# First gate and value weights converted inside the attention plan, in the last head pair's buffers

## The chip, the cores and the metric

The kernel runs on one core of a Trainium2 chip. The time is device microseconds (us) of one execution. An engine is named as in the profile: PE is the matrix engine (PEld its weight loads), DVE the vector engine, ACT the scalar engine, POOL the GpSimd engine, SP the engine that issues the DMAs. Each engine executes its own list of instructions from top to bottom, and waits at an instruction until what it needs is done.

## The reference, cut to what matters

```python
# attention: q, k, v are (2, 8, 1152, 64); queries are averaged in pairs
q_pool = q.reshape(B, H, S // 2, 2, D).mean(axis=3)
attn = softmax(q_pool @ k.T / sqrt(D));  attn_out = attn @ v
x = attn_out.transpose(0, 2, 1, 3).reshape(1152, 512)
# first mixture layer: w_gate, w_val are 512 x 1536, w_out is 1536 x 512, all float64
x = (sigmoid(x @ w_gate) * (x @ w_val)) @ w_out
# second layer: 8 experts, w1 512 x 1024, w2 1024 x 512, routing by 8 rounds of normalisation
out = sum(P[:, e:e+1] * (maximum(x @ w1[e], 0) @ w2[e]) for e in range(8))
```

## The kernel before

**Precision.** Every operand of a matmul is held as two words, a rounded high one and a low one with the rest. A product takes three matmuls (`three`, L902 to L905): high by high, high by low of the moving side, low weight by high. In the profile these three are L903, L904 and L905.

**Stages.** The attention runs over 8 head pairs of 9 query tiles each; PE turns and multiplies, DVE takes maxima and splits the turned probabilities (pT, L523), ACT exponentiates and copies, POOL rescales and writes the outputs as high and low words into x1 (tiles of four, one for each 128 columns of x; the last pair writes the last one). Then the gate and value stage runs over 12 blocks of 128 columns (`fc`). A block is 72 matmuls: 36 for the gate into one psum tile psb, 36 for the value into another (two such tiles in all, so block fc+1 uses those of block fc again). ACT takes the sigmoid of the first psb (L942), DVE multiplies it with the second psb (sg, L943), ACT writes the high word of the product (gt, L946) and POOL the low word (gt, L947). Then come the product with w_out and the eight experts.

**Converting float64 weights.** The weights arrive as 64-bit numbers and are turned into two float32 words by `split_doubles` (L184 to L217), for each of gate and value: ACT scales the upper halves (dv, L204), DVE cuts out the sign (ds, L205) and shifts (dv, L206), ACT rounds to the high word (w_gv, L210), DVE subtracts (da, L211), masks (dv, L212) and scales the lower halves (ds, L214), POOL adds both into the low word (w_gv, L217). Five DVE instructions, two of ACT, one of POOL. The results lie in a ring of two weight tiles; `dv` lies in SBUF for block 0 and in psum for the others.

**What sets the order.** The attention's instructions are steps with planned costs and due times; `arrange` (from L225) takes them one after the other by the earliest modelled start, hands out buffers of `stock`, and writes each engine's list in that order (L891 to L896). A step may be taken ahead of its turn by at most AHEAD = 8 units, one unit being a query tile. The gate and value stage is written as plain loops; there the framework's scheduler orders each engine's list by the priority of program order and its own estimates. Block 0's conversion has a raised priority (HP and HO, L923), by which it is mixed into the end of the attention.

Of the kernel before, what the change touches and what calls it, by code (L numbers as in the profile page):

```python
# [8 lines left out]
F32 = mybir.dt.float32  # L9
F32R = mybir.dt.float32r  # L10
I32 = mybir.dt.int32
U32 = mybir.dt.uint32
AF = mybir.ActivationFunctionType
ALU = mybir.AluOpType
AX = mybir.AxisListType
PSUM = bass.MemoryType.PSUM
P = 128
SIGN = -(1 << 31)
SIGNEXP = -(1 << 23)
RINGB = 2  # L20
RT0 = 24
RTS = 12
HP = 1
HO = 30
WA = 336
AHEAD = 8.0
SHIFT = {
# [99 lines left out]
def moe_stack_kernel(ctx: ExitStack, tc: tile.TileContext, q, k, v, wg1, wv1, wo1, wg2, w1, w2, out):  # L127
# [6 lines left out]
    nc = tc.nc  # L134
    B, H, S, D = q.shape
    SP = S // 2
    N, DM = out.shape
    wg1, wv1, wo1 = (w.bitcast(I32) for w in (wg1, wv1, wo1))
    FF = wo1.shape[0]
    E, _, FE = w1.shape  # L140
    KD = DM // P
    NJ = S // P
    NP = H // 2
# [6 lines left out]
    TB = N // 3  # L150
# [13 lines left out]
    def f(ap):  # L164
        return ap.bitcast(F32)
# [15 lines left out]
        j = eng.tensor_tensor(out=out[:, 1], in0=src, in1=f(out[:, 0]), op=ALU.subtract).ins  # L181
        return i, j

    def split_doubles(w, srcs, name, psum=None):  # L184

        for i, src in enumerate(srcs):
            raw = rawp.tile([P, 512, 2], I32, tag="raw", name=f"raw_{name}{i}")
            nc.sync.dma_start(out=raw.rearrange("p (a c) w -> p a (c w)", a=src.shape[1]), in_=src)
            low, high = raw[:, :, 0], raw[:, :, 1]
            a = conv.tile([P, 512], F32, tag="da", name=f"da_{name}{i}")
            s = conv.tile([P, 512], I32, tag="ds", name=f"ds_{name}{i}")
            if psum:
                v = psum.tile([P, 512], F32, tag="dv", name=f"dv_{name}{i}")
            else:  # L200
                v = conv.tile([P, 512], F32, tag="dv", name=f"dv_{name}{i}")
            vi = v.bitcast(I32)

            nc.scalar.activation(out=v, in_=f(high), func=AF.Copy, scale=2.0 ** -112)  # L204
            nc.vector.tensor_scalar(out=s, in0=vi, scalar1=SIGN, scalar2=None, op0=ALU.bitwise_and)  # L205
            nc.vector.scalar_tensor_tensor(  # L206
                out=vi, in0=vi, scalar=3, in1=s, op0=ALU.logical_shift_left, op1=ALU.bitwise_or
            )
            sl = slice(i * 512, (i + 1) * 512)
            nc.scalar.activation(out=w[:, 0, sl], in_=v, func=AF.Copy)  # L210
            nc.vector.tensor_tensor(out=a, in0=v, in1=f(w[:, 0, sl]), op=ALU.subtract)  # L211
            nc.vector.tensor_scalar(out=vi, in0=vi, scalar1=SIGNEXP, scalar2=None, op0=ALU.bitwise_and)  # L212
            t = f(s)
            nc.vector.scalar_tensor_tensor(  # L214
                out=t, in0=low.bitcast(U32), scalar=2.0 ** -52, in1=v, op0=ALU.mult, op1=ALU.mult
            )
            nc.gpsimd.tensor_tensor(out=w[:, 1, sl], in0=a, in1=t, op=ALU.add)  # L217

    x_p = ctx.enter_context(tc.tile_pool(name="x", bufs=1, reuse_waits="tile"))
    conv = ctx.enter_context(tc.tile_pool(name="conv", bufs=2, reuse_waits="tile"))  # L220
# [82 lines left out]
    U = 2 * QT + 1  # L303

    with ExitStack() as pa:
        ld = pa.enter_context(tc.tile_pool(name="ld", bufs=1, reuse_waits="tile"))
# [36 lines left out]
        have = {}  # L343
        steps = {}

        def step(name, eng, when, takes, lasts, emit, deps=(), takes_buf=(), frees=(), after=()):


            entry(steps, name, eng, when, takes, lasts, emit, deps, takes_buf, frees, after)
# [255 lines left out]
        for i in range(B * NP):  # L605
# [59 lines left out]
            for part in range(3):  # L665
                t = (-8.85, -1.45, -2.5)[part] if i == 0 else t0 - 8 + (0.4, 0.8, 0.0)[part]
                n = QT if part < 2 else 1
                made = ("pq", i, part if i == 0 or part == 2 else 3)
                if (i, part) == (0, 0):

                    for x, ts in enumerate((range(1), range(1, QT))):
                        c, w, tt = slice(ts[0] * P, (ts[-1] + 1) * P), len(ts) * P, t + 0.05 * x
# [30 lines left out]
            for j in range(2):  # L703
# [43 lines left out]
                t = t0 + 4.5 + 4 * j  # L747
# [140 lines left out]
            "wl", "POOL", t + 0.001, 150, 200,  # L888
            lambda: nc.gpsimd.tensor_tensor(out=wgs[:, :, 1], in0=wg2_sb, in1=f(wgs[:, :, 0]), op=ALU.subtract), ["wh"],
        )  # L890
        engines = {nc.tensor.engine, nc.vector.engine, nc.scalar.engine, nc.gpsimd.engine, nc.sync.engine}  # L891
        with tc.manual_schedule(engines=engines):
            for s in arrange(steps, stock, AHEAD):
                for what, kind, slot in s["got"]:
                    have[what] = stock[kind][slot]
                s["emit"]()  # L896


    rawp = ctx.enter_context(tc.tile_pool(name="raw", bufs=3, reuse_waits="tile"))
# [17 lines left out]
    with ExitStack() as pb:  # L917
        ring = pb.enter_context(tc.tile_pool(name="ring", bufs=RINGB, reuse_waits="tile"))
        g_p = pb.enter_context(tc.tile_pool(name="g", bufs=1, reuse_waits="tile"))
        gs = []  # L920
        for fc in range(NFF):
            w = ring_tile(f"gv{fc}")[:, :, 0:1024]
            with (tc.high_priority(offset=HO) if fc < HP else ExitStack()):  # L923
                split_doubles(
                    w,
                    [src[:, fc * 2 * P:(fc + 1) * 2 * P].rearrange("(c p) f -> p c f", p=P) for src in (wg1, wv1)],
                    f"gv{fc}", ps_v if fc else None,
                )
            wr = w.rearrange("p s (i c f) -> p s i c f", i=2, c=KD)
            pss = []  # L930
            for i in range(2):
                ps = ps_b.tile([P, 3, 512], F32, tag="b", name="psb")
                for c in range(KD):
                    for n in range(3):
                        cols = slice(n * TB, (n + 1) * TB)
                        three(
                            ps[:, n, 0:TB], wr[:, 0, i, c], wr[:, 1, i, c],
                            x1[c][:, 0, cols], x1[c][:, 1, cols], c == 0, c == KD - 1,
                        )
                pss.append(ps)  # L940
            sg = misc.tile([P, 3, TB], F32, tag="m", name="sg")
            nc.scalar.activation(out=sg, in_=pss[0][:, :, 0:TB], func=AF.Sigmoid)  # L942
            nc.vector.tensor_tensor(out=sg, in0=pss[1][:, :, 0:TB], in1=sg, op=ALU.mult)  # L943
            gt = g_p.tile([P, 2, N], F32R, tag=f"g{fc}", name="gt")
            sgf = sg.rearrange("p n w -> p (n w)")
            nc.scalar.activation(out=gt[:, 0], in_=sgf, func=AF.Copy)  # L946
            nc.gpsimd.tensor_tensor(out=gt[:, 1], in0=sgf, in1=f(gt[:, 0]), op=ALU.subtract)  # L947
            gs.append(gt)

        xa = [x_p.tile([P, 2, 2, HT], F32R, tag=f"x{u}", name=f"xa{u}") for u in range(2)]
        xb = [x_p.tile([P, 2, 2, HT], F32R, tag=f"x{2 + u}", name=f"xb{u}") for u in range(2)]
        xs = []

        def take_x(c, ps):
            xc = misc.tile([P, N], F32, tag="m", name="xs")
            nc.scalar.activation(out=xc.rearrange("p (n w) -> p n w", n=3), in_=ps[:, :, 0:TB], func=AF.Copy)
            xs.append(xc)
            if c % 2 == 0:  # L960
                x12, x11 = xc[:, 0:HT], xc[:, HT:N]
                split_x(xa[c // 2][:, 0], x11)
                nc.vector.tensor_tensor(out=x11, in0=x12, in1=x11, op=ALU.subtract)
                split_x(xa[c // 2][:, 1], x11)

        for c in range(KD):
            u, h = divmod(c, 2)
            w = ring_tile(f"o{c}")[:, :, 0:NFF * P]
            split_doubles(
                w,  # L970
                [
                    wo1[g * GRP * P:(g + 1) * GRP * P, c * 2 * P:(c + 1) * 2 * P].rearrange("(a p) e -> p a e", p=P)
                    for g in range(NFF // GRP)
                ],
                f"o{c}", ps_v,
            )
            if c < KD - 1:
                ps = ps_b.tile([P, 3, 512], F32, tag="b", name="pso")
                thirds = [ps[:, n, 0:TB] for n in range(3)]
            else:  # L980
                pbs.close()
                ps_f = ctx.enter_context(tc.tile_pool(name="ps_f", bufs=1, space=PSUM, reuse_waits="tile"))
                bank = {
                    k: ps_f.tile([P, 512], F32, tag=k, name=f"ps{k[0]}")
                    for k in ("B0", "B1", "X0", "Y1", "y0", "y1", "X1", "Y0")
                }
                thirds = [bank[k][:, 0:TB] for k in ("Y1", "y0", "y1")]
            for fc in range(NFF):
                wt = w[:, :, fc * P:(fc + 1) * P]
                for n in range(3):  # L990
                    cols = slice(n * TB, (n + 1) * TB)
                    three(
                        thirds[n], wt[:, 0], wt[:, 1], gs[fc][:, 0, cols], gs[fc][:, 1, cols],
                        fc == 0, fc == NFF - 1,
                    )
            if c < KD - 1:
                take_x(c, ps)
# [596 lines left out]
```

## Time and profile before

| | |
|---|---|
| median of 3 runs | 1262.05 us (1258.96, 1262.05, 1262.74) |
| profiled execution, its own time | 1260.09 us |
| its span, first to last instruction | 1258.3 us |
| attention ends, first matmul of the gate and value stage | 286.19 us |
| first matmul of its block 1 | 304.25 us |
| mean granted PE clock | 0.998 of full speed |
| PE, DVE, ACT, POOL busy | 98%, 85%, 62%, 57% of the span |

The window view gives busy time of each engine in a stretch and the granted PE clock as a share of full speed. A matmul's duration overlaps the next one's; the pace of PE is read from the starts. The wait view names for each idle time the instruction that ended it.

### The profile page before, as it was taken

To read this page: it belongs to the slowest core of one execution; us is meant where nothing else is said; L and a number is where in the kernel's file an instruction comes from. 1 tells how busy PE (TensorE), PEld (TensorE's weight loads), DVE (VectorE), ACT (ScalarE), POOL (GpSimd) and SP (SyncE) were. 2 spreads that over 40 slices of the span, in tenths; PEclk is the share of its full clock that TensorE was granted. 3 is DMA by queue.
4 is the path that set the end of the run, shared out by engine and by line. 5 is a ranking of instruction groups with operands and counts; after the bars stand their busy time and mean duration, and the time that the engine had idled before them with its cause. 6 is when DMAs were issued, how large, how long until landed. Compare 5 with 4: busy or idle time off the path is not lost.

```text
span 1258.3 us, 23700 instructions
## 1 busy us (share of the span) xinstructions
PE 1237.8 (98%) x8924; PEld 1205.8 (96%) x8924; DVE 1073.8 (85%) x1954; ACT 780.3 (62%) x1775; POOL 715.8 (57%) x751
## 2 busy tenths in 40 slices
PE   7999999998999999999999999999999999999998
PEld 6889999998999999999999999999999999999998
DVE  7999999997656674899998898898889889889887
ACT  7999999984333332756457457547556645745753
POOL 7788888664343432763464565564555556456552
PEclk9999999999999999999999999999999999999999
DMA  5112210113232332111111111111111110111112
GB/s 160 41 56 57 58 48 21 37 35 93 75 99 70 101 98 70 35 38 48 34 52 52 51 44 42 51 51 47 39 51 52 51 52 35 51 51 51 35 34 77
DMA packets 61204, 70.50 MB, mean 56 GB/s; under 512 B 3360, under 2 KB 47776, under 8 KB 61088
## 3 DMA queue, kind: packets, MB, share of 16 engines
q1 hardware_dynamic: 61088, 68.97, 17.8%
q8 instruction: 70, 1.15, 0.4%
q14 instruction: 46, 0.38, 0.1%
HBM read 66.60 MB, written 2.36 MB: 55 GB/s over the span
## 4 chain that ended last, share of the span: by engine, by line
PE 79%; DVE 12%; ACT 4%; POOL 2%; issue 2%; DMA 1%; SPq 0%; DVEq 0%; ACTq 0%; POOLq 0%
PE psb L905 4%; PE psb L904 4%; PE psb L903 4%; PE psY L903 4%; PE psY L904 4%; PE psY L905 4%; PE psX L903 4%; PE psX L904 3%; PE psX L905 3%; PE psX L1320 3%; PE psX L1325 3%; PE psX L1324 3%; PE psY L1320 3%; PE psY L1325 3%; PE psY L1324 3%; PE psg L542 3%
## 5 line engine op out<-in xcount | busy, mean ns | idle before, releaser
L1060 POOL TENSOR_TENSOR sm<-xs 128x512 f32<-128x512 f32 x64 | 92.5, 1457 | 165.9 <-ACT xs L1057 151.6
L1057 ACT ACTIVATE w_two<-sm 128x512 fp32r<-128x512 f32 x128 | 77.8, 629 | 163.7 <-POOL sm L1060 142.0
L1060 POOL TENSOR_TENSOR sm<-raw_w 128x256 f32<-128x256 f32 x128 | 105.4, 844 | 126.9 <-DMA raw_w<-in_moe_w_dram 84.7
L542 PE MATMUL psg<-pT,vs 128*128 128x256 f32 (+1 forms) x576 | 133.0, 318 | 0.1
L1060 DVE TENSOR_TENSOR hb<-sm,hb 128x512 fp32r<-128x512 f32 x128 | 119.5, 961 | 9.0 <-ACT hb L1057 9.0
L1060 DVE TENSOR_TENSOR w_two<-sm,w_two 128x512 fp32r<-128x512 f32 x128 | 112.7, 888 | 5.9 <-ACT w_two L1057 5.6
L1057 ACT ACTIVATE hb<-sm 128x512 fp32r<-128x512 f32 x128 | 75.9, 626 | 54.7 <-POOL sm L1060 53.5
L1320 PE MATMUL psX<-w_two,hb 128*128 128x256 f32 x384 | 108.8, 283 | 0.2 <-DVE acc L1276 0.2
L1320 PE MATMUL psY<-w_two,hb 128*128 128x256 f32 x384 | 108.5, 283 | 0.0
L523 DVE TENSOR_TENSOR pT<-psg,pT 128x384 fp32r<-128x384 f32 x192 | 102.0, 551 | 7.4 <-ACT pT L519 5.5
L1324 PE MATMUL psX<-w_two,hb 128*128 128x256 f32 x384 | 108.2, 282 | 0.0
L1324 PE MATMUL psY<-w_two,hb 128*128 128x256 f32 x384 | 108.2, 282 | 0.0
L1325 PE MATMUL psX<-w_two,hb 128*128 128x256 f32 x384 | 108.1, 281 | 0.1
L1325 PE MATMUL psY<-w_two,hb 128*128 128x256 f32 x384 | 108.0, 281 | 0.0
L503 PE MATMUL psg<-ident,p 128*128 128x128 f32 x648 | 104.4, 273 | 0.9 <-DVE pT L523 0.3
L905 PE MATMUL psb<-x,w_gv 128*128 128x384 f32 x288 | 96.9, 336 | 3.6 <-POOL w_gv L217 3.6
L903 PE MATMUL psb<-x,w_gv 128*128 128x384 f32 x288 | 97.0, 337 | 0.0
L904 PE MATMUL psb<-x,w_gv 128*128 128x384 f32 x288 | 96.9, 336 | 0.0
L542 PEld LDWEIGHTS psg<-pT,vs 128*128 128x128 f32 x576 | 91.2, 189 | 3.5 <-DVE pT L523 0.5
L519 ACT ACTIVATE pT<-psg 128x384 fp32r<-128x384 f32 x192 | 90.2, 496 | 6.1 <-PE psg L503 4.6
L1060 POOL TENSOR_TENSOR sm<-raw_w,sm 128x256 f32<-128x256 f32 x96 | 93.1, 983 | 0.3
L1060 DVE TENSOR_TENSOR hb<-xs,hb 128x512 fp32r<-128x512 f32 x96 | 88.8, 937 | 0.0
(266 smaller groups left out, 4691.1 us busy)
## 6 DMA issues: line engine op xcount, KB each, us to landing
raw_w<-in_moe_w_dram SPq DMA_DIRECT2D x64, 512.0 KB, 3.5
raw_gv<-in_moe_w_gate_dram SPq DMA_DIRECT2D x12, 512.0 KB, 3.5
raw_gv<-in_moe_w_val_dram SPq DMA_DIRECT2D x12, 512.0 KB, 3.5
raw_o<-in_moe_w_out_dram SPq DMA_DIRECT2D x12, 512.0 KB, 3.5
vr<-in_v_dram SPq DMA_DIRECT2D x16, 288.0 KB, 2.8
kr<-in_k_dram SPq DMA_DIRECT2D x15, 288.0 KB, 2.9
qr<-in_q_dram SPq DMA_DIRECT2D x15, 256.0 KB, 3.4
out_dram<-acc SPq DMA_DIRECT2D x8, 256.0 KB, 2.3
```

The lines of the kernel that those rows point to most:

```text
L503: nc.tensor.transpose(have["tpp", i, u, g][:, n * P:(n + 1) * P], have["p", i, u][:, jj * P:(jj + 1) * P], ident)
L519: nc.scalar.activation(out=p_parts(i, u, g)[0], in_=turned(i, u, g), func=AF.Copy)
L523: nc.vector.tensor_tensor(out=lo, in0=turned(i, u, g), in1=f(hi), op=ALU.subtract)
L542: nc.tensor.matmul(have["pv", i, j, n][:, 0:HALF[n][1]], have["vs", i, j][:, jj].rearrange("p a d -> p (a d)"), have["pT", i, j, n][s][:, ...
L903: nc.tensor.matmul(ps, wh, xh, start=first, stop=False, skip_group_check=more)
L904: nc.tensor.matmul(ps, wh, xl, start=False, stop=False, skip_group_check=more)
L905: return nc.tensor.matmul(ps, wl, xh, start=False, stop=last, skip_group_check=more).ins
L1057: nc.scalar.activation(out=out_, in_=in_, func=func)
L1060: eng.tensor_tensor(out=out_, in0=a, in1=b, op=op)
L1320: nc.tensor.matmul(out_, h[:, 0, cols], w[:, 0], start=(begins and kk + m == 0), stop=False, skip_group_check=True,)
L1324: nc.tensor.matmul(out_, h[:, 0, cols], w[:, 1], start=False, stop=False, skip_group_check=True)
L1325: nc.tensor.matmul(out_, h[:, 1, cols], w[:, 0], start=False, stop=(m == 1), skip_group_check=True)
```

## The change

The conversion of block 0's gate and value weights becomes two groups of steps in the attention plan (`convert`). The gate group is due 3 units before the end of the attention's last unit, the value group at that end. Their raw weights are loaded into the last pair's query buffers (qr, qs), their two words are written into the buffers of its split keys (ks), and `dv`, `ds` and `da` lie in SBUF. The first block's matmuls read the weights there (`first`). Block 0 still takes a tile of the ring, which nothing writes. HP, HO and the SBUF form of `dv` in `split_doubles` go.

```diff
@@ -20,8 +20,6 @@
 RINGB = 2
 RT0 = 24
 RTS = 12
-HP = 1
-HO = 30
 WA = 336
 AHEAD = 8.0
 SHIFT = {
@@ -181,7 +179,7 @@
         j = eng.tensor_tensor(out=out[:, 1], in0=src, in1=f(out[:, 0]), op=ALU.subtract).ins
         return i, j
 
-    def split_doubles(w, srcs, name, psum=None):
+    def split_doubles(w, srcs, name, psum):
 
 
 
@@ -195,10 +193,7 @@
             low, high = raw[:, :, 0], raw[:, :, 1]
             a = conv.tile([P, 512], F32, tag="da", name=f"da_{name}{i}")
             s = conv.tile([P, 512], I32, tag="ds", name=f"ds_{name}{i}")
-            if psum:
-                v = psum.tile([P, 512], F32, tag="dv", name=f"dv_{name}{i}")
-            else:
-                v = conv.tile([P, 512], F32, tag="dv", name=f"dv_{name}{i}")
+            v = psum.tile([P, 512], F32, tag="dv", name=f"dv_{name}{i}")
             vi = v.bitcast(I32)
 
             nc.scalar.activation(out=v, in_=f(high), func=AF.Copy, scale=2.0 ** -112)
@@ -888,12 +883,78 @@
             "wl", "POOL", t + 0.001, 150, 200,
             lambda: nc.gpsimd.tensor_tensor(out=wgs[:, :, 1], in0=wg2_sb, in1=f(wgs[:, :, 0]), op=ALU.subtract), ["wh"],
         )
+        def flat(x):
+            if isinstance(x, tuple):
+                x = x[0]
+            return x.rearrange("p a b c -> p (a b c)")[:, 0:1024]
+
+        def convert(k, src, raw_kind, t):
+
+            raw, wide = ("raw", k), ("wide", k)
+            v, sg, a = (conv.tile([P, 512], F32, tag=tag, name=f"{tag}_gv0{k}") for tag in ("dv", "ds", "da"))
+            vi, si = v.bitcast(I32), sg.bitcast(I32)
+            words = lambda: flat(have[raw]).bitcast(I32).rearrange("p (c w) -> p c w", w=2)
+            w = lambda x: flat(have[wide])[:, x * 512:(x + 1) * 512]
+
+            def load():
+                nc.sync.dma_start(
+                    out=flat(have[raw]).bitcast(I32).rearrange("p (a c) -> p a c", a=KD),
+                    in_=src[:, 0:2 * P].rearrange("(c p) f -> p c f", p=P),
+                )
+
+            def low():
+                nc.vector.scalar_tensor_tensor(
+                    out=sg, in0=words()[:, :, 0].bitcast(U32), scalar=2.0 ** -52, in1=v, op0=ALU.mult, op1=ALU.mult
+                )
+
+            n = lambda x: ("cv", k, x)
+            step(n("ld"), "SP", t - 6, 500, 3500, load, [], [(raw_kind, raw)])
+            step(
+                n("v"), "ACT", t, 530, 640,
+                lambda: nc.scalar.activation(out=v, in_=f(words()[:, :, 1]), func=AF.Copy, scale=2.0 ** -112), [n("ld")],
+            )
+            step(
+                n("s"), "DVE", t + 0.01, 345, 430, lambda: nc.vector.tensor_scalar(
+                    out=si, in0=vi, scalar1=SIGN, scalar2=None, op0=ALU.bitwise_and
+                ), [n("v")],
+            )
+            step(
+                n("x"), "DVE", t + 0.02, 600, 690, lambda: nc.vector.scalar_tensor_tensor(
+                    out=vi, in0=vi, scalar=3, in1=si, op0=ALU.logical_shift_left, op1=ALU.bitwise_or
+                ), [n("s")],
+            )
+            step(
+                n("h"), "ACT", t + 0.03, 530, 640, lambda: nc.scalar.activation(out=w(0), in_=v, func=AF.Copy), [n("x")],
+                [("ks", wide)],
+            )
+            step(
+                n("a"), "DVE", t + 0.04, 600, 690,
+                lambda: nc.vector.tensor_tensor(out=a, in0=v, in1=f(w(0)), op=ALU.subtract), [n("h")],
+            )
+            step(
+                n("e"), "DVE", t + 0.05, 345, 430, lambda: nc.vector.tensor_scalar(
+                    out=vi, in0=vi, scalar1=SIGNEXP, scalar2=None, op0=ALU.bitwise_and
+                ), [n("a")],
+            )
+            step(n("t"), "DVE", t + 0.06, 600, 690, low, [n("e")])
+            step(
+                n("l"), "POOL", t + 0.07, 1250, 1290,
+                lambda: nc.gpsimd.tensor_tensor(out=w(1), in0=a, in1=sg, op=ALU.add), [n("t"), n("a")],
+            )
+
+        t = U * B * NP
+        convert(0, wg1, "q", t - 3.0)
+        convert(1, wv1, "qs", t)
+
         engines = {nc.tensor.engine, nc.vector.engine, nc.scalar.engine, nc.gpsimd.engine, nc.sync.engine}
         with tc.manual_schedule(engines=engines):
             for s in arrange(steps, stock, AHEAD):
                 for what, kind, slot in s["got"]:
                     have[what] = stock[kind][slot]
                 s["emit"]()
+        first = [
+            flat(have["wide", k]).rearrange("p (s c f) -> p s c f", s=2, c=KD) for k in range(2)
+        ]
 
 
     rawp = ctx.enter_context(tc.tile_pool(name="raw", bufs=3, reuse_waits="tile"))
@@ -920,13 +981,15 @@
         gs = []
         for fc in range(NFF):
             w = ring_tile(f"gv{fc}")[:, :, 0:1024]
-            with (tc.high_priority(offset=HO) if fc < HP else ExitStack()):
+            if fc:
                 split_doubles(
                     w,
                     [src[:, fc * 2 * P:(fc + 1) * 2 * P].rearrange("(c p) f -> p c f", p=P) for src in (wg1, wv1)],
-                    f"gv{fc}", ps_v if fc else None,
-                )
-            wr = w.rearrange("p s (i c f) -> p s i c f", i=2, c=KD)
+                    f"gv{fc}", ps_v,
+                )
+                wr = [w.rearrange("p s (i c f) -> p s i c f", i=2, c=KD)[:, :, i] for i in range(2)]
+            else:
+                wr = first
             pss = []
             for i in range(2):
                 ps = ps_b.tile([P, 3, 512], F32, tag="b", name="psb")
@@ -934,7 +997,7 @@
                     for n in range(3):
                         cols = slice(n * TB, (n + 1) * TB)
                         three(
-                            ps[:, n, 0:TB], wr[:, 0, i, c], wr[:, 1, i, c],
+                            ps[:, n, 0:TB], wr[i][:, 0, c], wr[i][:, 1, c],
                             x1[c][:, 0, cols], x1[c][:, 1, cols], c == 0, c == KD - 1,
                         )
                 pss.append(ps)
```

Where it moves instructions. First DVE, at the passage from attention to gate and value stage; before, from the last DVE step of block 1's gate on (numbers behind names are buffers: 3797 to 3799 block 1's gate, 3810 to 3812 its value, 3904 to 3906 and 3917 to 3919 block 2):

```order
L214 SCALAR_TENSOR_TENSOR ds_gv_3798<-raw_gv_3795,dv_gv_3799 128x512
L206 SCALAR_TENSOR_TENSOR dv_gv_3812<-dv_gv_3812,ds_gv_3811 128x512
L205 TENSOR_SCALAR ds_gv_3905<-dv_gv_3906 128x512
L211 TENSOR_TENSOR da_gv_3810<-dv_gv_3812,w_gv_3794 128x512
L212 TENSOR_SCALAR dv_gv_3812<-dv_gv_3812 128x512
L206 SCALAR_TENSOR_TENSOR dv_gv_3906<-dv_gv_3906,ds_gv_3905 128x512
L214 SCALAR_TENSOR_TENSOR ds_gv_3811<-raw_gv_3808,dv_gv_3812 128x512
L205 TENSOR_SCALAR ds_gv_3918<-dv_gv_3919 128x512
L206 SCALAR_TENSOR_TENSOR dv_gv_3919<-dv_gv_3919,ds_gv_3918 128x512
L943 TENSOR_TENSOR sg<-psb,sg 128x1152
L211 TENSOR_TENSOR da_gv_3904<-dv_gv_3906,w_gv_3901 128x512
```

Now, the same place (3795 to 3797 is block 1's gate, 3808 to 3810 its value):

```order
L587 TENSOR_TENSOR sw_143<-psg_147,sw_143 64x64
L200 TENSOR_SCALAR ds_gv_3796<-dv_gv_3797 128x512
L200 TENSOR_SCALAR ds_gv_3809<-dv_gv_3810 128x512
L201 SCALAR_TENSOR_TENSOR dv_gv_3797<-dv_gv_3797,ds_gv_3796 128x512
L201 SCALAR_TENSOR_TENSOR dv_gv_3810<-dv_gv_3810,ds_gv_3809 128x512
L1006 TENSOR_TENSOR sg<-psb,sg 128x1152
L206 TENSOR_TENSOR da_gv_3795<-dv_gv_3797,w_gv_3792 128x512
L207 TENSOR_SCALAR dv_gv_3797<-dv_gv_3797 128x512
L206 TENSOR_TENSOR da_gv_3808<-dv_gv_3810,w_gv_3792 128x512
L209 SCALAR_TENSOR_TENSOR ds_gv_3796<-raw_gv_3793,dv_gv_3797 128x512
```

The product sg of block 0 stood behind the whole conversion of block 1; now it stands ahead of the last three DVE steps of that conversion.

POOL at the same passage, before (w_gv_3687 is block 0, w_gv_3794 block 1, w_gv_3901 block 2; x_3 is the last tile of x1):

```order
L217 TENSOR_TENSOR w_gv_3687<-da_gv_3690,ds_gv_3691 128x512
L168 TENSOR_SCALAR x_3_79<-sw_143 64x320
L600 TENSOR_TENSOR x_3_79<-sw_143,x_3_79 64x320
L217 TENSOR_TENSOR w_gv_3687<-da_gv_3703,ds_gv_3704 128x512
L217 TENSOR_TENSOR w_gv_3794<-da_gv_3797,ds_gv_3798 128x512
L217 TENSOR_TENSOR w_gv_3794<-da_gv_3810,ds_gv_3811 128x512
L947 TENSOR_TENSOR gt<-sg,gt 128x1152
L217 TENSOR_TENSOR w_gv_3901<-da_gv_3904,ds_gv_3905 128x512
```

And now (ks_121 holds block 0's value weights, w_gv_3792 is block 1, w_gv_3899 block 2):

```order
L942 TENSOR_TENSOR ks_121<-da_gv_156,ds_gv_155 128x512
L166 TENSOR_SCALAR x_3_79<-sw_143 64x320
L595 TENSOR_TENSOR x_3_79<-sw_143,x_3_79 64x320
L1010 TENSOR_TENSOR gt<-sg,gt 128x1152
L212 TENSOR_TENSOR w_gv_3792<-da_gv_3795,ds_gv_3796 128x512
L212 TENSOR_TENSOR w_gv_3792<-da_gv_3808,ds_gv_3809 128x512
L212 TENSOR_TENSOR w_gv_3899<-da_gv_3902,ds_gv_3903 128x512
```

The low word of block 0's product (gt) has moved from behind both low words of block 1's weights to ahead of them.

PE where block 1 begins, now (L964 to L966 are the three matmuls of a product; the second pair of rows belongs to the value's psb):

```order
L966 MATMUL psb<-x_3_79,ks_121 128x384
L964 MATMUL psb<-x_0_76,w_gv_3792 128x384 [waits Activation_49]
L965 MATMUL psb<-x_0_76,w_gv_3792 128x384
L964 MATMUL psb<-x_0_76,w_gv_3792 128x384 [waits DVE_49,Activation_49]
L965 MATMUL psb<-x_0_76,w_gv_3792 128x384
L966 MATMUL psb<-x_0_76,w_gv_3792 128x384 [waits Pool_49]
```

Before, the third matmul of block 1 was the first that waited for POOL; now two matmuls of the value half stand ahead of it, and it is the fifth.

## Rows read from the trace of the kernel before

**Rows 1.** The page: busy time of each engine, share of the span, instructions.

```profile
PE 1237.8 (98%) x8924; PEld 1205.8 (96%) x8924; DVE 1073.8 (85%) x1954; ACT 780.3 (62%) x1775; POOL 715.8 (57%) x751
```

**Rows 2.** Waits of PE, whole span: total us, times, longest us.

```profile
PE psb L905 <- POOL w_gv L217: 3.6, 1, 3.6
```

**Rows 3.** Timeline, PE, start of the gate and value stage: start us, us, instruction.

```profile
286.19 0.42 PE L903 MATMUL psb<-x,w_gv 128*128 128x384 f32 x1
286.45 0.34 PE L904 MATMUL psb<-x,w_gv 128*128 128x384 f32 x1
290.43 0.44 PE L905 MATMUL psb<-x,w_gv 128*128 128x384 f32 x1 [3.64 <-POOL w_gv L217]
...
294.71 0.34 PE L905 MATMUL psb<-x,w_gv 128*128 128x384 f32 x1
```

**Rows 4.** Windows of block 0: length, busy us (instructions), clock, DMA share, GB/s.

```profile
286.19:290.43 4.24, 0.60 (x6) 0.28 (x3) 4.12 (x7) 1.59 (x3) 2.33 (x3) 1.00 0.06 10
290.43:294.71 4.28, 4.28 (x15) 4.28 (x16) 3.49 (x7) 1.14 (x2) 3.03 (x3) 0.60 0.74 232
294.71:304.25 9.54, 9.54 (x56) 9.54 (x56) 6.61 (x11) 4.26 (x5) 2.58 (x2) 1.00 0.36 111
```

**Rows 5.** Timeline, all engines, end of block 0 and what follows it.

```profile
304.08 0.33 PE L905 MATMUL psb<-x,w_gv 128*128 128x384 f32 x1
304.25 0.33 PE L903 MATMUL psb<-x,w_gv 128*128 128x384 f32 x1
...
304.45 1.36 DVE L943 TENSOR_TENSOR sg<-psb,sg 128x1152 f32<-128x1152 f32 x1 [0.84 <-PE psb L905]
...
305.84 1.17 ACT L946 ACTIVATE gt<-sg 128x1152 fp32r<-128x1152 f32 x1 [0.22 <-DVE sg L943]
...
307.09 2.69 POOL L947 TENSOR_TENSOR gt<-sg,gt 128x1152 fp32r<-128x1152 f32 x1 [4.94 <-ACT gt L946]
...
307.52 0.68 DVE L214 SCALAR_TENSOR_TENSOR ds_gv<-raw_gv,dv_gv 128x512 f32<-128x512 uint32 x1
...
309.73 1.30 POOL L217 TENSOR_TENSOR w_gv<-da_gv,ds_gv 128x512 fp32r<-128x512 f32 x1
```

**Rows 6.** Window of the last head pair: PE, PEld, DVE, ACT, POOL as in rows 4.

```profile
250.70:282.20 31.50, 30.73 (x230) 29.09 (x230) 30.08 (x70) 28.38 (x76) 21.93 (x32) 1.00 0.10 34
```

**Rows 7.** Timeline, DVE, last head pair and the conversion of block 0.

```profile
257.68 0.56 DVE L523 TENSOR_TENSOR pT<-psg,pT 128x384 fp32r<-128x384 f32 x1 [0.75 <-ACT pT L519]
...
281.18 1.02 DVE L523 TENSOR_TENSOR pT<-psg,pT 128x384 fp32r<-128x384 f32 x2
282.12 0.41 DVE L589 TENSOR_TENSOR sw<-psg,sw 64x256 f32<-64x256 f32 x1
...
284.80 0.43 DVE L589 TENSOR_TENSOR sw<-psg,sw 64x256 f32<-64x256 f32 x1
285.26 0.69 DVE L206 SCALAR_TENSOR_TENSOR dv_gv<-dv_gv,ds_gv 128x512 int32<-128x512 int32 x1
285.87 0.89 DVE L211 TENSOR_TENSOR da_gv<-dv_gv,w_gv 128x512 f32<-128x512 f32 x1
...
287.31 0.43 DVE L212 TENSOR_SCALAR dv_gv<-dv_gv 128x512 int32<-128x512 int32 x1
287.65 0.69 DVE L211 TENSOR_TENSOR da_gv<-dv_gv,w_gv 128x512 f32<-128x512 f32 x1
288.26 0.69 DVE L214 SCALAR_TENSOR_TENSOR ds_gv<-raw_gv,dv_gv 128x512 f32<-128x512 uint32 x1
...
289.43 1.22 DVE L212 TENSOR_SCALAR dv_gv<-dv_gv 128x512 int32<-128x512 int32 x1
```

**Rows 8.** Timeline, POOL, first low word and the last words of x1.

```profile
289.11 1.26 POOL L217 TENSOR_TENSOR w_gv<-da_gv,ds_gv 128x512 fp32r<-128x512 f32 x1 [1.77 <-DVE ds_gv L214]
291.07 0.88 POOL L168 TENSOR_SCALAR x<-sw 64x320 fp32r<-64x320 f32 x1 [0.70 <-DVE sw L592]
...
292.04 0.86 POOL L600 TENSOR_TENSOR x<-sw,x 64x320 fp32r<-64x320 f32 x1
```

## The prediction, on record before the kernel ran

> **What bounds the kernel now.** I read the page first, then the waits of PE, and then the timeline and the windows at the place that the waits name. PE is busy 98% of the span, DVE 85% [rows 1]. Once the attention is under way, the largest wait of PE is one single stall, 3.6 us for a low weight word that POOL writes [rows 2]. It lies at the first products of the gate and value stage [rows 3]: two matmuls start at 286.19 and 286.45, the third, the first with the low word, at 290.43. The windows then show a mean granted clock of 0.60 for 4.28 us, a mixture of 1.2 and 2.4 GHz, and 1.00 before and after [rows 4]. At full clock 55 matmuls start in 9.54 us, 0.1735 us apiece [rows 4].
>
> So the start costs this much: 17 steps of 0.1735 us after 286.19 the eighteenth matmul would start at 289.14; it starts at 294.71 [rows 3], 5.57 us late. Of these, 3.89 are the wait (290.43 less 286.54), and 1.68 the low clock (15 steps in 4.28 us instead of 2.60). Behind it PE runs without a gap to the end of the stage, so whatever is won or lost here goes into the end time in full.
>
> **What the change removes.** Block 0's gate words are finished about three units earlier, its value words near the end of the attention. The wait for the low word at 290.43 and the low clock behind it go: minus 5.57 us.
>
> **What it puts into the attention.** In the last pair DVE is busy 30.08 us of 31.50, and PE 30.73 [rows 6]; both are near their limit. Ahead of the last pT (it ends at 282.20 [rows 7]) one DVE step of the conversion was done; now six are. The five additional ones, by start to start in rows 7: shift 0.61 (285.26 to 285.87), subtract 0.61 (287.65 to 288.26), mask 0.34 (287.31 to 287.65), scale 0.69, and one more sign cut that I price as the mask; 2.59 us. The one usable gap in the pair is 0.75 us ahead of 257.68 [rows 7]. The last pT then ends at 282.20 + 2.59 - 0.75 = 284.04; with 0.2 us for longer instructions (below) 284.2.
>
> From there to the first product stand eight small DVE steps (two divisions, a shift, two sums, two reciprocals, an addition). In before a like set, an AND in the place of one sum with reciprocal, ran from 282.12 to 284.80 [rows 7], 2.68 us; a wake and PE's three turns add about 0.3 us. The last pT ends 0.08 after the first of these starts, so the first product starts at 284.2 - 0.08 + 2.68 + 0.3 = 287.1, less some 0.15 because the sum and reciprocal are shorter than the AND: 286.95, against 286.19. I charge 0.8 us. Bounds: -0.5 (PE's own small waits in that pair vanish and DVE finds more gaps) and +2.6 (each added instruction is stretched).
>
> The stretch is seen where DVE works on SBUF beside POOL: the mask took 0.43 us at 287.31 and 1.22 us at 289.43 [rows 7], while POOL's 1.26 us addition ran [rows 8]; the subtract at 285.87 took 0.89 against 0.69. Five steps by 0.2 to 0.8 us each are 1 to 4 us if all meet POOL; in the last pair POOL is busy 21.93 of 31.50 us [rows 6], but a step is stretched only by the overlapping part, and the wait must fall on the path, hence my 0.2. The Trainium skill, page "SBUF — State Buffer", section "SBUF: two separate sides", says that DVE and GpSimd share one pair of ports as an exclusive lock, and that the later one is blocked for the whole instruction when the DVE instruction has two SBUF inputs or a two-port mode. The 1.22 us row agrees; by the rule every one of the five could stand behind a whole POOL instruction, which is the slow rival below.
>
> ACT gets one activation of 128x512 more ahead of the last copies, in a pair in which it is busy 28.38 of 31.50 us [rows 6]; its spare 3.1 us cover it, and DVE is the later one: 0 (up to 0.6, half of the 1.17 us that 128x1152 takes in rows 5). POOL's low word of the gate stands between two rescalings, and its DVE input is finished several maxima earlier: 0. The two loads move to the front of SP's list, behind loads that wait for buffers freed earlier: 0.
>
> **The last words of x1.** POOL now writes the value's low word ahead of the last two x1 steps. DVE finishes the value's scaling about 2.2 us after the last reciprocal (subtract, division, mask, addition, scale), near 289.1; POOL takes 1.26, then 0.97 to the next start and 0.86 [rows 8], so x1 is complete near 292.3. The matmuls that need it are the 34th and 35th of the block, 286.95 + 33 x 0.1735 = 292.7. It fits by 0.3 us: 0 (0 to 1).
>
> **What takes the place of the wait.** The order shows that DVE now multiplies block 0's product (sg) before the last three steps of block 1's conversion, and that POOL writes the product's low word (gt) before block 1's first low weight word. Both lists are executed in order, so block 1's low word cannot come before this chain: last matmul of block 0, sg, ACT's gt, POOL's gt, POOL's w_gv. The trace of before has the same five instructions in a row, with block 2's word at the end [rows 5]: the last matmul starts at 304.08, sg at 304.45, ACT at 305.84, POOL at 307.09, w_gv at 309.73. In rows 3 and 8 PE goes on 1.32 us after such an addition starts (289.11 to 290.43). That is 309.73 + 1.32 - 304.08 = 6.97 us after the last matmul. DVE's own three steps end at 308.2 [rows 5] and hide behind POOL's gt. In before the word at the end was not needed until block 2. Now PE can place four matmuls of block 1, and the fifth, due 5 x 0.1735 = 0.87 us after the last of block 0, waits: 6.97 - 0.87 = 6.10 us.
>
> Then the clock. A PE idle for 3.6 us ran the next stretch at a mean of 0.60 [rows 3, 4]; here it is idle for about 1.3 and 4.7 us with two matmuls between. I charge the same 1.68 us (0 if it does not fall, up to 3.4 if the low stretch is twice as long). Together plus 7.78 us. Block 1's value word follows 1.3 us later and is needed after 34 more matmuls; block 2 not for another 72 x 0.1735 = 12.5 us. No further wait.
>
> **Sum.** -5.57 + 0.8 + 0 + 7.78 = +3.0 us. The stall has moved from block 0 to block 1, and grown. The profiled execution took 1260.09 us, 2 us less than the median of the three runs, 1262.05; the sum of terms is made in its trace and gives 1263.1 there. I set it on the median: 1265.0 us.
>
> **Rivals.**
>
> *The new stall does not form* (the order of sg and gt does not bind, because block 0's product is done early or block 1's words come some other way). Then -5.57 + 0.8 = -4.8, 1257.3 us. For it: once x1 is done, near 292, DVE has nothing to do until block 0 ends (286.95 + 72 x 0.1735 = 299.4), long enough for the conversion. Against it: the two lists.
>
> *DVE is overloaded in the last pair.* Place: the five conversion steps between the last pair's maxima and pT; price: with 2 us of stretch the last pT ends at 286.0 instead of 284.2, the first product at 288.8, and the sum is +4.9, 1267 us. It decides for slower from the point at which the first product starts after 287.7 (+1.5 instead of +0.8). For it: DVE at 30.08 of 31.50 us, the row of 1.22 us; against it: PE can run the value products of finished tiles while DVE is late, and most DVE steps there read psum, not SBUF.
>
> *The change does not do what it says*: the gate's low word is still late at the first product, as the steps may slip behind others. Then the old wait stays beside the new one, +7 us and more, 1269. Against it: the gate's POOL step stands ahead of three rescalings of the last pair.
>
> **How the numbers follow.** Forecast 0.70, no stall 0.10, overloaded DVE 0.17, no effect 0.03. The forecast's own range, from the bounds of the clock and of the last pair, is 1262.5 to 1267.5. About 0.3% of the time, 3.8 us, is what a measurement of this kernel can tell from no change. Within the forecast some 0.25 lie above +3.8; with the two slow rivals slower is 0.36; faster is most of the no-stall case, 0.07; the same 0.57. The range for 8 in 10 is 1259 to 1268.5: it takes in half of the no-stall case's spread and most of the overloaded one.
>
> **What would show it.** PE's wait for w_gv at the third matmul of block 0 is gone; a wait of 4 to 5 us for w_gv at the fifth matmul of block 1, with POOL's gt just ahead of it; a granted clock below 1.00 after that, and not around 290 us; the first product between 286.2 and 287.7. It would be wrong if PE showed no wait at block 1, or one behind block 1 as well, or if the first product came after 288.

## The result, and the profile after

The changed kernel takes 1274.38 us (median of 6 runs, 1271.51 to 1275.63), the kernel before 1258.99 beside it (6 runs). The ratio on record is 1.0108, with a 95% interval of 1.0097 to 1.012; the two medians alone give 1.0122. The forecast was 1265.0, with a range of 1259 to 1268.5: the sign was right, the size was not.

PE's waits over the whole span, changed kernel (total us, times, longest us):

```profile
PE psX L964 <- ACT w_two L1120: 4.9, 1, 4.9
PE psb L966 <- POOL w_gv L212: 4.5, 1, 4.5
...
PE psX L966 <- DVE w_two L1123: 0.8, 1, 0.8
...
PE psb L964 <- ACT w_gv L205: 0.7, 1, 0.7
...
PE psb L964 <- DVE sg L1006: 0.2, 1, 0.2
```

The three waits at psb, two for block 1's words and a short one for sg to set a psb free, make up the stall that was forecast. The wait for w_two was not: it lies at the first product of the expert stage (psX), 219 us later.

PE, from the first product of block 0 into block 1:

```profile
286.66 0.42 PE L964 MATMUL psb<-x,ks 128*128 128x384 f32 x1
286.92 0.34 PE L965 MATMUL psb<-x,ks 128*128 128x384 f32 x1
287.09 0.34 PE L966 MATMUL psb<-x,ks 128*128 128x384 f32 x1
...
299.05 0.34 PE L966 MATMUL psb<-x,ks 128*128 128x384 f32 x1
300.13 0.44 PE L964 MATMUL psb<-x,w_gv 128*128 128x384 f32 x1 [0.73 <-ACT w_gv L205]
300.40 0.34 PE L965 MATMUL psb<-x,w_gv 128*128 128x384 f32 x1
300.99 0.41 PE L964 MATMUL psb<-x,w_gv 128*128 128x384 f32 x1 [0.25 <-DVE sg L1006]
301.25 0.34 PE L965 MATMUL psb<-x,w_gv 128*128 128x384 f32 x1
306.08 0.69 PE L966 MATMUL psb<-x,w_gv 128*128 128x384 f32 x1 [4.50 <-POOL w_gv L212]
306.56 0.52 PE L964 MATMUL psb<-x,w_gv 128*128 128x384 f32 x1
306.88 0.52 PE L965 MATMUL psb<-x,w_gv 128*128 128x384 f32 x1
```

The third matmul, which started 3.98 us after the second [rows 3], now follows after 0.17. Block 0 runs dense to 299.05; the fifth matmul of block 1 starts 7.03 us later (worked out ahead: 6.97), and the next are 0.32 apart instead of 0.17, at a granted clock of 0.50 (window: length, then PE, PEld, DVE, ACT, POOL busy, granted clock, DMA share, GB/s):

```profile
306.08:309.40 3.32, 3.32 (x10) 3.32 (x11) 2.66 (x5) 1.14 (x2) 1.28 (x1) 0.50 0.29 78
```

What stands ahead of it, all engines, answering to [rows 5]:

```profile
299.48 1.08 ACT L205 ACTIVATE w_gv<-dv_gv 128x512 fp32r<-128x512 f32 x2 [5.16 <-PE psb L966]
299.49 1.36 DVE L1006 TENSOR_TENSOR sg<-psb,sg 128x1152 f32<-128x1152 f32 x1 [6.54 <-issue]
300.88 1.17 ACT L1009 ACTIVATE gt<-sg 128x1152 fp32r<-128x1152 f32 x1 [0.32 <-DVE sg L1006]
302.19 2.62 POOL L1010 TENSOR_TENSOR gt<-sg,gt 128x1152 fp32r<-128x1152 f32 x1 [9.80 <-ACT gt L1009]
304.77 1.26 POOL L212 TENSOR_TENSOR w_gv<-da_gv,ds_gv 128x512 fp32r<-128x512 f32 x1
```

Sg, ACT's gt, POOL's gt and w_gv follow each other as forecast. But ACT's high words of block 1 also start only at 299.48, after 5.16 us of waiting for a matmul of block 0, though DVE had written their input near 293. No row ahead of the prediction speaks of that.

The entry of the expert stage: ACT's copies, PE, then the windows (columns as above):

```profile
505.41 0.69 ACT L1120 ACTIVATE x<-xs 128x576 fp32r<-128x576 f32 x1 [0.52 <-PE psy L966]
...
519.25 0.63 PE L1515 MATMUL psB<-xa 128*128 128x512 f32 x2
519.50 0.72 ACT L1120 ACTIVATE w_one<-raw_w 128x256 fp32r<-128x256 f32 x2 [13.40 <-PE psy L966]
...
524.76 0.61 PE L964 MATMUL psX<-xa,w_two 128*128 128x288 f32 x1 [4.88 <-ACT w_two L1120]
```

```profile
524.76:531.20 6.44, 5.63 (x22) 5.28 (x23) 6.36 (x10) 5.38 (x12) 1.63 (x2) 0.50 0.27 81
531.20:535.00 3.80, 3.80 (x30) 3.80 (x30) 3.14 (x4) 3.40 (x9) 0.63 (x1) 0.97 0.00 0
```

Before, the copy of w_one stood right behind that of x, and PE began the experts without a wait (ACT, then PE):

```profile
502.57 0.69 ACT L1057 ACTIVATE x<-xs 128x576 fp32r<-128x576 f32 x1 [0.52 <-PE psy L905]
503.16 0.71 ACT L1057 ACTIVATE w_one<-raw_w 128x256 fp32r<-128x256 f32 x2
...
516.88 0.30 PE L903 MATMUL psX<-xa,w_two 128*128 128x288 f32 x1
```

Now w_one waits for the last product with w_out (psy, near 519), and w_two behind it is late. Then PE runs at a granted clock of 0.50, which is 1.2 GHz, for 6.4 us.

The start of the attention (its first 18 us) takes up to 2.5 us more in one execution than in another, so stages are compared by lengths: from one turn of a sum in the attention (244.72 in before, 243.80 after) to the first product of block 0, from there to the first product with w_out (pso), to the first of the experts (psX), to the end. All columns are us. E5's own profiled execution took 1335.40 us at a mean granted clock of 0.85, so its row is read from e8, the same kernel once more.

| kernel | attention end | gate and value | w_out | experts | together | median, ratio |
|---|---|---|---|---|---|---|
| before | 41.47 | 155.34 | 75.35 | 741.42 | 1013.58 | |
| changed | 42.86 | 157.71 | 80.39 | 744.94 | 1025.90 | 1274.38, 1.0108 |
| e4_before_place | 41.46 | 153.80 | 80.38 | 745.78 | 1021.42 | 1269.14, 1.0073 |
| e1_place | 42.88 | 158.56 | 75.34 | 741.37 | 1018.15 | 1263.49, 1.0037 |
| e2_early1 | 42.86 | 156.09 | 80.39 | 744.53 | 1023.87 | 1272.16, 1.0100 |
| e3_both | 42.87 | 156.08 | 75.34 | 741.85 | 1016.14 | 1262.78, 1.0025 |
| e5_swap, e8_swap_look | 42.86 | 158.84 | 75.34 | 741.17 | 1018.21 | 1264.55, 1.0035 |
| e6_swap_early1 | 42.85 | 149.84 | 75.34 | 741.07 | 1009.10 | 1255.52, 0.9963 |
| e7_due | 47.97 | 149.87 | 75.34 | 740.95 | 1014.13 | 1261.68, 1.0013 |

The change costs 12.32 us in this table, and 15.4 us by the medians: its profiled execution, 1271.51, is the shortest of its six, at a mean granted clock of 0.994, and the four longest have 0.992 to 0.993. The 12.32 are +1.39 at the end of the attention, +2.37 in the gate and value stage, and 5.04 + 3.52 = 8.56 at the entry of the experts.

### The profile page after: what moved, and what is told of

The parts are those of the page before. It is cut to its first block, busy times and chain, and to the rows that moved or that the text cites. A ratio compares the mean times of both kernels' runs of the same rounds, so it can differ in the third digit from the quotient of the medians.

```text
span 1269.7 us, 23704 instructions
## 1 busy us (share of the span) xinstructions
PE 1242.3 (98%) x8924; PEld 1208.4 (95%) x8924; DVE 1068.8 (84%) x1954; ACT 780.1 (61%) x1775; POOL 715.1 (56%) x751
## 4 chain that ended last, share of the span: by engine, by line
PE 78%; DVE 13%; ACT 4%; issue 2%; POOL 2%; DMA 1%; SPq 0%; DVEq 0%; ACTq 0%; POOLq 0%
PE psb L966 4%; PE psY L964 4%; PE psb L964 4%; PE psb L965 4%; PE psY L965 4%; PE psY L966 4%; PE psX L964 4%; PE psX L966 3%; PE psX L965 3%; PE psX L1383 3%; PE psX L1388 3%; PE psX L1387 3%; PE psY L1383 3%; PE psY L1388 3%; PE psY L1387 3%; DVE pT L518 3%
## 5 line engine op out<-in xcount | busy, mean ns | idle before, releaser
L966 PE MATMUL psb<-x,w_gv 128*128 128x384 f32 x264 | 89.1, 338 | 4.5 <-POOL w_gv L212 4.5
L964 PE MATMUL psb<-x,w_gv 128*128 128x384 f32 x264 | 89.1, 338 | 1.0 <-ACT w_gv L205 0.7
L965 PE MATMUL psb<-x,w_gv 128*128 128x384 f32 x264 | 88.9, 337 | 0.0
L1123 DVE TENSOR_TENSOR w_two<-raw_w,w_two 128x512 fp32r<-128x512 f32 x96 | 73.0, 762 | 18.0 <-ACT w_two L1120 16.3
```

Source lines behind the costliest of these rows:

```text
L964: nc.tensor.matmul(ps, wh, xh, start=first, stop=False, skip_group_check=more)
L965: nc.tensor.matmul(ps, wh, xl, start=False, stop=False, skip_group_check=more)
L966: return nc.tensor.matmul(ps, wl, xh, start=False, stop=last, skip_group_check=more).ins
L1123: eng.tensor_tensor(out=out_, in0=a, in1=b, op=op)
```

## The experiments

**Where the buffers lie.** The two built programs differ in one more thing than the order: the addresses (bytes of a partition).

| tile | before | changed | e1 |
|---|---|---|---|
| w_gv0 | 82752 to 97088 | none | none |
| w_gv1, gv3, ..., w_o1, w_o3 | 97088 to 111424 | 82752 to 97088 | as changed |
| w_gv2, gv4, ..., w_o0, w_o2 | 82752 to 97088 | 97088 to 111424 | as changed |
| w_one (two), first two w_two | 82752 to 95040 | 82752 to 95040 | 99136 to 111424 |
| ks (two; now block 0's words) | 84800 to 94016 | 84800 to 94016 | as changed; in e5 and e6 107840 to 117056 |

The ring has two places, taken in turn. Block 0's tile is still asked for, but nothing writes it, and it is not in the program at all: every later tile has changed places. The last weights of the stage, w_o3, now lie where w_one goes, and block 1's where block 0's words are read. E4 puts w_one at 99136 too, but there the ring has its turn of before, so w_one comes to lie over w_o3. That gives theory A (w_one waits for w_o3's readers) and later theory D (block 1's words wait for the readers of ks).

**e1_place and e4_before_place: the place of w_one.** One edit, in the changed kernel and in the kernel before:

```diff
+    two = lambda k: w_p.tile([P, 2, 2, 2, P], F32R, tag=f"w2{k}", name="w_two")
+    late = [two(k) for k in (2, 3, 4, 5)]
     stock = {
...
-        "w2": [w_p.tile([P, 2, 2, 2, P], F32R, tag=f"w2{k}", name="w_two") for k in range(9)],
+        "w2": [two(k) for k in (0, 1)] + late + [two(k) for k in (6, 7, 8)],
```

> The changed kernel with one edit: the four w_two buffers that the expert stage needs last are placed first, so that w_one and the first w_two lie over the ring buffer of the third output block (w_o2) again and not over that of the fourth and last (w_o3). Theory A (block 0 no longer takes a ring buffer, so the turn of the two ring buffers is exchanged to the end of the stage, and the first expert weights must wait for the last output product): no PE wait for w_two at the start of the expert stage, ACT's first w_one copy right behind its x copy; 8.6 us faster than the changed kernel's 1274.4, so 1265.8 (1264 to 1268); the wait at the fifth matmul of block 1 stays at 4.5 us. Rival B (the wait for w_two is only a consequence of the stall in block 1, which shifts the expert stage against its loads and conversions): 1274.4, and the wait of 4.9 us stays.

> The kernel before, with the placement alone: the four late w_two buffers are placed first, which here puts w_one and the first w_two over the ring buffer of the last output block, w_o3. Block 0 and all orders are those of before. Theory A: a PE wait of 4 to 5.5 us for w_two at the start of the expert stage, low clock behind it, 8.6 us slower than before: 1267.6 (1265 to 1270). Rival B: no difference, 1259.

Measured: e1 1263.49 (ratio 1.0037, 95% interval 1.0024 to 1.005), just under the range expected; e4 1269.14 (1.0073, 1.0059 to 1.0087), inside its own. In e1 the wait at the fifth matmul of block 1 is still 4.5 us, and ACT copies w_one at once:

```profile
508.73 0.69 ACT L1122 ACTIVATE x<-xs 128x576 fp32r<-128x576 f32 x1 [0.52 <-PE psy L966]
509.32 0.71 ACT L1122 ACTIVATE w_one<-raw_w 128x256 fp32r<-128x256 f32 x2
```

In e4, where nothing ahead of the experts is changed, the wait appears (ACT, then PE):

```profile
502.27 0.69 ACT L1059 ACTIVATE x<-xs 128x576 fp32r<-128x576 f32 x1 [0.52 <-PE psy L905]
516.36 0.72 ACT L1059 ACTIVATE w_one<-raw_w 128x256 fp32r<-128x256 f32 x2 [13.40 <-PE psy L905]
...
521.62 0.40 PE L903 MATMUL psX<-xa,w_two 128*128 128x288 f32 x1 [4.88 <-ACT w_two L1059]
```

The idle time of ACT is 13.40 us in both kernels with this place, the one of PE 4.88. In the table the last two columns add 8.62 in e1's favour and 9.39 to e4's loss; theory A holds from both sides, and rival B falls: the wait does not come from the lateness of the stage before.

**e2_early1 and e3_both: the order.** Block 1's conversion gets the priority that block 0's had:

```diff
             if fc:
-                split_doubles(
+                with (tc.high_priority(offset=30) if fc < 2 else ExitStack()):
+                    split_doubles(
...
```

> The changed kernel with one edit: block 1's conversion has the priority that block 0's had before, so that its steps stand ahead of block 0's sg on DVE and its low words ahead of gt on POOL; nothing else moves. Theory A: no wait at the third and fifth matmul of block 1 and no low clock behind it, 7.7 us less (6.2 of lateness, 1.5 of low clock); the wait of 4.9 us for w_two at the expert stage stays, since the buffers lie as in the changed kernel: 1266.7 (1265 to 1269). Rival B (the expert wait comes from the lateness): both waits go, about 1258. Rival C (the stall in block 1 is not the order of sg and gt but a buffer that the attention releases late, since w_gv of block 1 also waits for PE): the wait at block 1 stays, 1274.

> Both edits together: block 1's conversion with priority, and the expert weights placed as to the ring buffers of before. Theory A: the two gains add, 1274.4 - 8.6 - 7.7 = 1258.1; by the sums of the trace (-5.6 for block 0 and +1.4 for the last head pair) it should be 4 us under before, 1255. I expect 1256.5 (1254 to 1259). Rival B: the same as the priority alone.

Measured: e2 1272.16 (1.0100, 1.0085 to 1.0114), e3 1262.78 (1.0025, 1.0015 to 1.0035), both above the ranges of theory A. The placement and this edit add, but the order alone gives 1.6 us (e2) and 2.5 (e3) in the gate and value stage, not 7.7. The edit also moved more than the expectation says: in the built program ACT's two high words of block 1 now stand ahead of block 0's sigmoid, not behind it, and the two matmuls of the value half no longer stand ahead of the third of block 1. The stall has moved to block 1's first matmul. ACT in e2, then PE there:

```profile
300.54 1.08 ACT L205 ACTIVATE w_gv<-dv_gv 128x512 fp32r<-128x512 f32 x2 [10.50 <-PE psb L966]
301.64 1.28 ACT L1006 ACT_TABLE_LOAD   x1
302.94 1.13 ACT L1006 ACTIVATE sg<-psb 128x1152 f32<-128x1152 f32 x1
...
304.12 0.44 PE L964 MATMUL psb<-x,w_gv 128*128 128x384 f32 x1 [3.67 <-ACT sg L1006]
```

The last matmul of block 0 starts at 300.11; only then may ACT write block 1's high words, after 10.50 us of idleness. Behind them wait the sigmoid and with it the psb that block 1 needs. This is near to rival C: a buffer holds block 1, only that block 0, not the attention, still reads the memory under block 1's ring tile. In the built program of the changed kernel this write waits for the last of block 0's 72 matmuls, although the high words (82752 to 86848) lie over the gate's ks alone, whose last matmul starts near 293: the wait is for the tile as a whole.

**e5_swap (its trace: e8_swap_look) and e6_swap_early1: both causes apart.** Block 0's words are moved from under block 1's tile (in the built program of e5 the high words wait for no matmul); e5 has e1's placement and on every engine the order of the changed kernel, e6 also e2's priority:

```diff
-            "ks": slots(prep, 2, [P, NJ, 2, D], F32R, "ks"),
             "kT": slots(prep, 3, [P, NJ * P], F32R, "kT"),
             "vs": slots(prep, 2, [P, NJ, 2, D], F32R, "vs"),
+            "ks": slots(prep, 2, [P, NJ, 2, D], F32R, "ks"),
```

> The changed kernel with the expert weights placed as in e1_place, and the two ks buffers, in which block 0's converted words now lie, placed behind kT and vs instead of ahead of them, so that they no longer share memory with block 1's ring buffer. The order of all instructions stays that of the changed kernel (sg and gt of block 0 ahead of block 1's last conversion steps). Theory D (two independent causes hold block 1, the order of sg and gt, and the memory of ks under its ring buffer; each alone is enough): ACT writes w_gv of block 1 early (near 295 us), yet the wait at the fifth matmul of block 1 stays near 4.5 us; as e1_place, 1263.5 (1262 to 1265). Rival E (the memory alone was the cause): the wait goes, 1256.5.

> The kernel of e5_swap once more, for its trace at full clock. Theory D: ACT writes block 1's high words near 296 us, while block 0's products still run, and PE waits 4.5 us for POOL's low word at the fifth matmul of block 1 all the same, since DVE's sg and POOL's gt stand ahead of it. Rival E: no wait there.

> As e5_swap, and block 1's conversion with the priority of e2_early1. Both causes of the stall at block 1 are gone, and the expert weights wait for nothing. Theory D: no PE wait at block 1, no low clock there; against e3_both 6.5 us less: 1256 (1254.5 to 1258), about 0.3% faster than before: -5.6 for block 0, +1.4 for the last head pair. Rival F (a third cause, for instance DVE or POOL too slow for block 1's words once they start near 292 us): a wait of 1 to 3 us at block 1, 1258 to 1261.

Measured: e5 1264.55 (1.0035, 1.0022 to 1.0049); e6 1255.52 (0.9963, 0.9951 to 0.9976); both inside the ranges of theory D. The kernel of e5, trace of e8, all engines:

```profile
294.90 1.08 ACT L205 ACTIVATE w_gv<-dv_gv 128x512 fp32r<-128x512 f32 x2
...
300.17 1.36 DVE L1006 TENSOR_TENSOR sg<-psb,sg 128x1152 f32<-128x1152 f32 x1 [6.54 <-issue]
302.93 2.62 POOL L1010 TENSOR_TENSOR gt<-sg,gt 128x1152 fp32r<-128x1152 f32 x1 [9.85 <-ACT gt L1009]
305.51 1.26 POOL L212 TENSOR_TENSOR w_gv<-da_gv,ds_gv 128x512 fp32r<-128x512 f32 x1
306.83 0.69 PE L966 MATMUL psb<-x,w_gv 128*128 128x384 f32 x1 [4.56 <-POOL w_gv L212]
```

The high words are there 5 us before block 0 ends, and the fifth matmul waits all the same, for sg and gt. With both edits, e6, PE passes from block 0 (ks) to block 1 (w_gv) without a gap:

```profile
299.74 0.33 PE L966 MATMUL psb<-x,ks 128*128 128x384 f32 x1
299.91 0.33 PE L964 MATMUL psb<-x,w_gv 128*128 128x384 f32 x1
300.08 0.33 PE L965 MATMUL psb<-x,w_gv 128*128 128x384 f32 x1
```

So there were two causes, and each alone held most of the stall: in the table the memory alone costs 156.08 - 149.84 = 6.24 us (e3), the order alone 9.00 (e8), both 8.72 (e1). The 6.24 hold for the order of e2, with the sigmoid behind the high words; the price of the memory in another order was not measured. Theory D holds. E6 is the fastest version, 0.37% under the kernel before.

**e7_due: the conversion earlier.**

```diff
-        convert(0, wg1, "q", t - 3.0)
-        convert(1, wv1, "qs", t)
+        convert(0, wg1, "q", t - 9.0)
+        convert(1, wv1, "qs", t - 5.0)
```

> As e6_swap_early1, with the conversions of block 0 due 6 (gate) and 5 (value) tile steps earlier, so that ten of their steps instead of six stand ahead of the last pT on DVE, and four fewer behind it. Theory G (DVE has no gaps in the last pairs, and each step of 0.35 to 0.6 us put ahead of the last pT delays it): the first product, 1.4 us later than before at the same point of the attention in the changed kernel, is 1.5 to 3 us later; 1256.5 to 1258. Rival H (earlier pairs have gaps for it): the first product is 0 to 1 us later than before, 1254.5 to 1255.5.

Measured: 1261.68 (1.0013, 1.0004 to 1.0022); the first product is 6.5 us later than before, 5.1 later than in e6. Theory G has the direction, but it said 1.5 to 3 us, less than half of what came. PE's waits up to the first product, the longest four:

```profile
PE psg L563 <- DVE pT L518: 1.4, 1, 1.4
PE psg L563 <- DVE sw L579: 1.2, 1, 1.2
PE psg L498 <- DVE pT L518: 0.8, 1, 0.8
PE psg L498 <- POOL p L490: 0.8, 1, 0.8
```

Most are for DVE. In this trace three of the conversion's DVE steps are stretched: the value's shift, mask and scaling take 1.85, 1.52 and 1.14 us, against 0.67, 0.43 and 0.69 at their shortest in the changed kernel. What the planner's other choice of steps adds was not taken apart.

## Why the prediction was wrong, by its steps

**Block 0's stall, -5.57.** Right. E6, in which nothing else of the stage is late, shortens the stage by 155.34 - 149.84 = 5.50. In e4, where the clock did not fall behind the same wait (last section), that stall costs 153.80 - 149.84 = 3.96.

**The last head pair, +0.8.** It was 1.39, inside the bounds. Counted from the same turn, the last pT ends 2.49 us later than before (forecast 2.0), and the first product follows 2.89 us after that end (forecast 2.75). The forecast gave 0.2 us for longer instructions. One step alone was stretched by more, just ahead of the last pT (changed kernel, DVE, POOL and PE):

```profile
280.61 1.48 POOL L533 TENSOR_TENSOR pT<-rem,pT 128x576 fp32r<-128x576 f32 x1
280.75 1.62 DVE L917 TENSOR_SCALAR ds_gv<-dv_gv 128x512 int32<-128x512 int32 x1
282.30 1.47 DVE L518 TENSOR_TENSOR pT<-psg,pT 128x384 fp32r<-128x384 f32 x3
282.98 2.43 PE L537 MATMUL psg<-pT,vs 128*128 128x320 f32 x15 [0.75 <-DVE pT L518]
```

The value's sign cut, priced at 0.34 like the mask [rows 7], took 1.62 us. It started 0.14 us after a POOL addition and ended 0.28 us after it; the last three pT stand behind it, and PE waits 0.75 us for them. The Trainium skill, page "SBUF — State Buffer", section "SBUF: two separate sides", says that whichever of DVE and GpSimd comes second is blocked for the whole instruction of the first, where the DVE instruction has a two-port mode or two SBUF inputs; this row agrees, though no run here shows in which mode the step ran. By that rule an estimate of the step, where it meets such an addition, is 1.48 - 0.14 + 0.43 = 1.77 us, 0.15 more than it took. The gate's sign cut took 1.35 us and ended 0.29 us after such an addition; the other four steps ahead of the last pT took at most 0.69.

**The last words of x1, 0.** Right: no wait in block 0.

**The new stall, +7.78.** The place, the fifth matmul and the size were right: 2.37 + 5.50 = 7.87. The lateness of the fifth matmul was 306.08 - 299.05 - 0.87 = 6.16 (forecast 6.10), and the rest, 1.71, is the low clock (forecast 1.68). That the clock's share fits is luck: in e1, after the same lateness, the stall costs 8.72 in all. The cause was named only in half. The lists of DVE and POOL do bind (e5), but ACT's high words could not have come earlier either (e2).

**The step that failed** is "Behind it PE runs without a gap to the end of the stage, so whatever is won or lost here goes into the end time in full", together with "No further wait" and the sentence of the section on the change that block 0 still takes a tile of the ring. PE does run without a gap to the end of the stage, and the 3.76 us that the terms so far add up to (+1.39 and +2.37; forecast +3.0) arrive there in full. But the change also took a tile out of the ring's turn, and so the expert stage's first weights had to wait for the last product with w_out. That is 8.56 us, in no term, no rival and no bound; e1 takes away 8.62 by the place alone. The prediction's own sign of being wrong, a wait behind block 1 as well, came true. Without this wait the time is that of e1, 1263.49, inside the range; partly by luck, since the forecast stood on 1262.05, the median of three executions of the kernel before, 3 us above the median of six. Where the memory of the next stage's first tiles lies, and which tiles are read there last, stood in the built program, and no step of the prediction asked for it.

## What to carry to other kernels

A change that takes one use out of a rotating buffer shifts all later uses: compare the addresses of the two built programs, and ask of every stage behind the change whose last reader lies under its first tiles. When a stall has one good explanation in an engine's order, look for a second in memory before pricing its removal; here each cause alone kept 6 to 9 us, and only both edits together paid. When words are put into freed buffers, the tile that would take that memory next inherits the wait.

## What the runs showed of the hardware

The same idle time does not always cost the same clock. Kernel before: a wait of 3.64 us, then a mean granted clock of 0.60 for 4.28 us [rows 3, 4]. E4, with the same instructions there and a wait of 3.66 (columns as above):

```profile
287.44:291.69 4.25, 0.59 (x5) 0.27 (x3) 4.12 (x7) 1.59 (x3) 2.35 (x3) 1.00 0.06 13
291.69:295.96 4.27, 4.27 (x24) 4.27 (x25) 3.48 (x7) 1.13 (x2) 3.05 (x3) 1.00 0.73 232
```

The clock stayed at 2.4 GHz, 24 matmuls instead of 15 fit, and the stage is 1.54 us shorter. The stall at block 1 shows the same: in the changed kernel and in e1 the fifth matmul waits 4.50 us, and the mean granted clock behind it is 0.75 over 6.92 us in the one and 0.62 over 6.95 us in the other; e1's stage is 0.85 us longer. The 1.68 us that the prediction took from [rows 4] as a price of the stall are one draw of something that varies between executions, and a single profile cannot tell which.
